# Three engines of a fused attention and two-MLP kernel: a fixed order for token blocks two to four, and the weight preparation in smaller parts

## The chip, the cores and the metric

The kernel runs on one core of a Trainium2 chip, as one launch. The metric is the device time of that launch in microseconds. Five engines work side by side on the core, each through its own queue: TensorE (PE in the profile, with the weight loads apart as PEld), VectorE (DVE), ScalarE (ACT), GpSimd (POOL, nearly unused here) and SyncE (SP), which issues nearly all DMAs.

## The reference, cut to what matters

Chunked attention with memory tokens makes `x`, an MLP with a leaky ReLU turns it into a second `x`, and a gated MLP makes the output. All arrays are float32; there are 3072 tokens of width 512.

```python
# _attn_ref: 4 batches, 8 heads, 768 positions of width 64, chunks of 32 that see 16 left, 8 right, 8 memory tokens
scores = scale * np.matmul(q_c, k_full.transpose(0, 1, 3, 2))
a = np.exp(scores - np.max(scores, axis=-1, keepdims=True))
out[:, :, c_start:c_end] = np.matmul(a / (np.sum(a, axis=-1, keepdims=True) + 1e-09), v_full)
# _moe_ref: w_in 512 x 2048, w_out 2048 x 512
h = x @ w_in
x2 = np.maximum(0.01 * h, h) @ w_out
# _moe2_ref: w_a, w_b 512 x 1536, w_out 1536 x 512
y = ((x2 @ w_a) * (x2 @ w_b)) @ w_out
```

## The kernel before

**Number format.** Every float32 operand of a matmul is split into a high and a low part, and each product takes three matmuls: `mm3` in the first layer (`h<-xh,w`, `h<-xl,w`, `h<-xh,w`) and the same in `mm2` (`a<-gh,w`, `a<-gl,w`, `a<-gh,w`). The high part is a ScalarE cast, the low part a VectorE subtraction.

**Token blocks and items.** The tokens are cut into six blocks of 512 (`NB3`). Blocks one to four (`NL` = 4, index `bi` 0 to 3) go through the first MLP plainly; blocks five and six go together through a Strassen form; the gated MLP follows for all. An item is one block with one of the 16 slices `f` of the inner width; this document numbers the items `16*bi + f`, so block two begins with item 16, block three with 32, block four with 48. The first block has three half items more (its items 16 to 18 of 256 tokens), so that its last half matmuls run beside the first items of block two.

**What an item does.** `mm1_pe` runs 12 matmuls into a PSUM tile `h` (pool `ps_h`, two buffers in turn). `mm1_act` runs two ScalarE operations on it, `g` (the leaky ReLU, which reads `h` and so gives the buffer back) and `gh` (the high part), and VectorE makes `gl`. `mm2` runs the 12 matmuls of the item two items back (`LAG` = 2) into four accumulators `a` (pool `ps_a`, four buffers, all of them used by one block). At the end of a block ScalarE copies the four accumulators out (`x<-a`), and only then the next block can accumulate.

**Attention beside it.** The attention of a later block is made in pairs of units (128 tokens) beside the items: at the items in `STARTS` the scores of a pair run (`s<-k,qz`, on PE), then the softmax, the 16 transposes per unit on VectorE (`pt<-p`), and at the next start the product with V (`pv<-pt,v`). The product uses the same two `h` buffers as the items, and its result goes to `xh` (ScalarE) and `xl` (VectorE).

**Weight preparation.** The weights of the gated MLP are prepared in the meantime, as 18 blocks of work (six pairs of slices, three matrices each). The generator `prep_steps` gives out four steps for each: twice load a tile `raw`, bias it on ScalarE and join its halves into `pz` on VectorE; then the ScalarE casts into `pwa` and four combinations `ps` and the low parts on VectorE; then the cast into `pwb`, its low part, and the stores `wab<-pwa`, `wab<-pwb` (or `wtd<-...`) to DRAM. `pz`, `pwa`, `ps` and `pwb` have one buffer each, `raw` has four, loaded three ahead. 49 of the 72 steps are spread evenly over the 48 items of blocks two to four (`STEPS, pace`), the rest goes to the Strassen part, three for each of its rounds.

**Order.** `InOrder` wraps an engine: while it is on, every instruction of that engine is held behind the one emitted before it. It is on for the first items and again from the Strassen part on. In between the framework's scheduler sets each engine's order. On the chip every engine runs its queue in the order in which it was built.

Of the kernel before, what the change touches and what calls it, by code (L numbers as in the profile page):

```python
# [28 lines left out]
NL = NB3 - 2  # L29
# [26 lines left out]
def kernel(  # L56
# [61 lines left out]
    def w_join_lo(lo, z):  # L118
        dve.scalar_tensor_tensor(
            z, lo, 29, z, ALU.logical_shift_right, ALU.bitwise_or  # L120
        )

    def w_parts(hi, lo, z, eng):

        act.copy(hi, z)
        eng.tensor_tensor(out=lo, in0=z, in1=hi.bitcast(F32), op=ALU.subtract)


# [559 lines left out]

    def next_pair(u):
        for k in (2, 3):  # L690
            q_place(u + k, nc.scalar.copy)
        q_load(u + 6)
        k_load(2 * u + 8)

# [15 lines left out]
    for k, i in enumerate(STARTS[:-1]):  # L710
        u = 2 * TB // UT + 2 * k
        for v in (u, u + 1):
            at_item(i, a_scores, v)
        at_item(i, next_pair, u)
        at_item(i, a_soft1, u)
        at_item(i, a_soft1, u + 1)
        at_item(i + 1, a_soft2, u)
        at_item(i + 2, a_turn, u)
        at_item(i + 2, a_soft2, u + 1)
        at_item(i + 3, a_turn, u + 1)  # L720

# [15 lines left out]

    def prep_join(n, z):
        prep_load(n + AHEAD)
        w_bias(raws[n])  # L740
        w_join(raws[n], z)

    def prep_steps():
        n = 0
        for p in range(NF2 // 2):
            for m in range(3):
                z = prep.tile([P, 2, 512], I32, tag="pz", name="pz", bufs=1)
                for k in range(2):
                    prep_join(n, z[:, k, :])
                    n += 1  # L750
                    yield
# [10 lines left out]
                t = prep.tile([P, 4, 256], F32, tag="ps", name="ps", bufs=1)  # L762

                def plain(c, n, src):
                    w_parts(
                        wa[:, c:c + n, 0], wa[:, c:c + n, 1],
                        src.rearrange("p (a n) -> p a n", n=256), dve,
                    )

                def plain4(c, src):  # L770
                    w_parts(*[
                        wa[:, c, l].rearrange("p (d a j) -> p d a j", d=2, j=32) for l in range(2)
                    ], src, dve)

                def comb(c, x, y, op):
# [7 lines left out]
                    dve.tensor_tensor(out=o, in0=x, in1=y, op=op)  # L783

                if m < 2:
                    plain(0, 2, z[:, 0, :])
                    plain(2, 1, z22)
                    comb(1, z21, z22, ALU.add)
                    comb(0, t[:, 1], z11, ALU.subtract)
                    comb(2, z11, z21, ALU.subtract)  # L790
                    comb(3, z12, t[:, 0], ALU.subtract)
                else:
                    plain4(0, z11)
                    plain4(1, z21)
                    plain4(2, z22)
                    comb(0, z12, z11, ALU.subtract)
                    comb(1, z22, t[:, 0], ALU.subtract)
                    comb(2, z22, z12, ALU.subtract)
                    comb(3, z21, t[:, 1], ALU.subtract)
                yield  # L800
                g, k = divmod(p, 2)
# [6 lines left out]
                wb = prep.tile([P, 4, 2, 256], F32R, tag="pwb", name="pwb", bufs=1)  # L808
                w_parts(wb[:, :, 0], wb[:, :, 1], t, dve)
                yield  # L810
                if m < 2:
                    nc.sync.dma_start(out=d[:, 2:5], in_=wb[:, 0:3].bitcast(F32))
                    nc.sync.dma_start(out=d[:, 6], in_=wb[:, 3].bitcast(F32))
                else:
                    nc.sync.dma_start(out=wtd[g][:, 3:7, k], in_=wb.bitcast(F32))

    steps = prep_steps()


# [165 lines left out]

    STEPS, pace = 49, 0.0
    for bi, f, parts in items[LEAD:]:
        first = bi == 0
        if f == 0 and not first:
            if bi + 1 < NL:  # L990
                x_tiles(("x", bi + 1))
            else:
                x_raw()
        if first:
            W1.load(2 * f + 14)
            W1.step()
        behind.append((bi, parts, mm1(bi, parts)))
        if first:
            W1.step()
        if len(behind) > LAG:  # L1000
            mm2(*behind.pop(0))
        for fn in beside.get((bi, f), []):
            fn()
        if not first:
            wo_load((bi - 1) * NF1 + f + 3)

            i = (bi - 1) * NF1 + f
            n = (NL - 1) * NF1
            pace += STEPS / n
            near = {i + NF1, i + NF1 - 1, i + NF1 + 1} & set(STARTS)  # L1010
            for _ in range(0 if near else int(pace)):
                pace -= 1
                next(steps, None)
        elif f >= NF1 - 1:
            wo_load(f - NF1 + 2)
            prep_load(f - NF1 + 1)


# [33 lines left out]

    for e in (pe, dve, act):
        e.on, e.last = True, None
    whole = slice(0, TB)
# [8 lines left out]
    for p in range(NF1 // 2):  # L1064
# [14 lines left out]
        prod(Bk, p, 1, 1, False)  # L1079
        if p:  # L1080
            next(steps, None)
        g11 = relu(Bk)()
# [16 lines left out]
        if p:  # L1099
            next(steps, None)  # L1100
        prod(A, p, 5, 2, False)
# [3 lines left out]
        if p:  # L1105
            next(steps, None)
        late = summed(u2, C)
# [520 lines left out]
```

## Time and profile before

| | |
|---|---|
| median of 3 runs | 1120.54 us (1120.48 to 1122.62) |
| the profiled execution | 1120.36 us |
| its span | 1118.5 us |
| what lies around the span | 1.86 us |
| PE busy | 1096.0 us (98% of the span) |
| DVE busy | 772.9 us (69%) |
| ACT busy | 526.6 us (47%) |
| granted TensorE clock | 0.998 |

The span runs from the first to the last instruction. PE busy counts the time in which at least one matmul is in flight, so what is missing from 100% is time in which TensorE had nothing to run. The stages lie in the span as follows: block one to about 128 us, blocks two to four to about 425 us, the Strassen part to about 553 us, then the last matmuls of blocks five and six and the gated MLP.

### The profile page before, as it was taken

To read this page: it belongs to the slowest core of one execution; us is meant where nothing else is said; L and a number is where in the kernel's file an instruction comes from. 1 tells how busy PE (TensorE), PEld (TensorE's weight loads), DVE (VectorE), ACT (ScalarE), POOL (GpSimd) and SP (SyncE) were. 2 spreads that over 40 slices of the span, in tenths; PEclk is the share of its full clock that TensorE was granted. 3 is DMA by queue.
4 is the path that set the end of the run, shared out by engine and by line. 5 is a ranking of instruction groups with operands and counts; after the bars stand their busy time and mean duration, and the time that the engine had idled before them with its cause. 6 is when DMAs were issued, how large, how long until landed. Compare 5 with 4: busy or idle time off the path is not lost.

```text
span 1118.5 us, 16332 instructions
## 1 busy us (share of the span) xinstructions
PE 1096.0 (98%) x6195; PEld 908.6 (81%) x6195; DVE 772.9 (69%) x1417; ACT 526.6 (47%) x893; POOL 7.4 (1%) x18
## 2 busy tenths in 40 slices
PE   7899999999999999999999999999999999999997
PEld 6788888888888888877788888888888888888886
DVE  6796388978898665778551737588736578745676
ACT  5887556664555235666622424144434243433232
POOL 2000000000000000000000000000000000000000
PEclk9999999999999999999999999999999999999999
DMA  9996889889998423556688756566877566767452
GB/s 315 404 345 229 282 308 344 297 337 365 327 325 335 158 81 135 186 200 226 246 329 290 266 191 201 181 211 193 275 229 219 166 220 192 242 182 242 143 185 76
DMA packets 99854, 270.63 MB, mean 242 GB/s; under 512 B 9664, under 2 KB 24128, under 8 KB 99008
## 3 DMA queue, kind: packets, MB, share of 16 engines
q1 hardware_dynamic: 98032, 267.88, 70.4%
q10 hardware_dynamic: 1744, 1.70, 0.5%
q8 instruction: 49, 0.80, 0.3%
q14 instruction: 29, 0.24, 0.1%
HBM read 215.02 MB, written 54.53 MB: 241 GB/s over the span
## 4 chain that ended last, share of the span: by engine, by line
PE 81%; DVE 9%; ACT 5%; DMA 3%; issue 1%; SPq 1%; DVEq 0%; ACTq 0%
PE ca L49 18%; PE cc L49 9%; PE oa L49 9%; PE a L49 7%; PE cb L49 5%; PE oy L49 4%; PE h L438 4%; PE a L562 4%; PE a L566 3%; PE a L565 3%; PE h L439 3%; PE h L440 3%; DVE pt L351 2%; PE A L49 2%; PE oz L49 1%; PE pv L391 1%
## 5 line engine op out<-in xcount | busy, mean ns | idle before, releaser
L49 PE MATMUL ca<-ch,wab 128*128 128x512 f32 x576 | 192.2, 389 | 0.0
L49 ACT CAST st<-gb 128x512 fp32r<-128x512 f32 x126 | 76.5, 621 | 124.5 <-DVE gb L49 123.9
L49 PEld LDWEIGHTS ca<-ch,wab 128*128 128x128 f32 x576 | 108.1, 188 | 23.2 <-ACT a L49 0.4
L49 PE MATMUL ca<-cl,wab 128*128 128x512 f32 x288 | 112.2, 389 | 0.0
L49 PE MATMUL oa<-st,wt 128*128 128x512 f32 x420 | 104.3, 389 | 0.0
L438 PE MATMUL h<-xh,w 128*128 128x512 f32 (+1 forms) x256 | 100.5, 393 | 2.8 <-DVE xl L425 2.1
L49 PE MATMUL cc<-ch,wab 128*128 128x512 f32 x288 | 100.3, 389 | 0.0
L439 PE MATMUL h<-xl,w 128*128 128x512 f32 (+1 forms) x256 | 98.6, 385 | 0.2 <-DVE xl L49 0.2
L440 PE MATMUL h<-xh,w 128*128 128x512 f32 (+1 forms) x256 | 98.5, 385 | 0.0
L562 PE MATMUL a<-gh,w 128*128 128x512 f32 (+1 forms) x256 | 97.7, 382 | 0.5 <-ACT x L580 0.5
L565 PE MATMUL a<-gl,w 128*128 128x512 f32 (+1 forms) x256 | 97.5, 381 | 0.0
L566 PE MATMUL a<-gh,w 128*128 128x512 f32 (+1 forms) x256 | 97.5, 381 | 0.0
L49 DVE TENSOR_TENSOR st<-gb,st 128x512 fp32r<-128x512 f32 x126 | 85.3, 689 | 15.0 <-ACT st L49 13.3
L49 PEld LDWEIGHTS oa<-st,wt 128*128 128x128 f32 x420 | 78.8, 188 | 16.4
L49 ACT COPY u<-ca 128x512 f32<-128x512 f32 x72 | 42.3, 587 | 91.5 <-PE ca L49 91.4
L351 DVE STREAM_TRANSPOSE pt<-p 32x128 f32<-32x128 f32 x256 | 77.4, 302 | 3.5
L49 PEld LDWEIGHTS cc<-ch,wab 128*128 128x128 f32 x288 | 54.1, 188 | 11.3
L49 PEld LDWEIGHTS ca<-cl,wab 128*128 128x128 f32 x288 | 54.1, 188 | 11.1
L530 ACT ACTIVATE g<-h 128x512 f32<-128x512 f32 (+1 forms) x64 | 37.3, 583 | 54.2 <-PE h L440 53.9
L536 DVE TENSOR_TENSOR gl<-g,gh 128x512 fp32r<-128x512 f32 (+1 forms) x64 | 43.0, 672 | 26.8 <-ACT gh L533 23.2
L438 PEld LDWEIGHTS h<-xh,w 128*128 128x128 f32 x256 | 48.1, 188 | 13.3 <-DVE xl L425 2.5
L562 PEld LDWEIGHTS a<-gh,w 128*128 128x128 f32 x256 | 48.1, 188 | 10.3 <-ACT x L580 0.9
(198 smaller groups left out, 2050.7 us busy)
## 6 DMA issues: line engine op xcount, KB each, us to landing
wab<-wab SPq DMA_DIRECT2D x126, 512.0 KB, 4.4
w<-wod SPq DMA_DIRECT2D x80, 512.0 KB, 5.3
raw<-w SPq DMA_DIRECT2D x68, 512.0 KB, 7.0
wt<-wtd SPq DMA_DIRECT2D x63, 512.0 KB, 4.5
k<-kl SPq DMA_DIRECT2D x48, 256.0 KB, 4.8
v<-vl SPq DMA_DIRECT2D x48, 256.0 KB, 5.6
wab<-pwb SPq DMA_DIRECT2D x12, 768.0 KB, 5.5
wod<-w SPq DMA_DIRECT2D x16, 512.0 KB, 6.8
```

The lines of the kernel that those rows point to most:

```text
L49: self.last = emit(*args, **kwargs).ins
L351: dve.transpose(out=pt[o0:o0 + 32, :, 2 * cpar + hpar, hpx, :], in_=p[i0:i0 + 32, hpx::2, 32 * b:32 * b + 32],)
L391: pe.matmul(o[64 * hpar:64 * hpar + 64, 2 * pair:2 * pair + 2, t0:t0 + CH], v[:, i:i + 64], pt[:, 2 * cp + pair, 2 * cpar + hpar].rearrang ...
L438: pe.matmul(ps, w[1], x[0], start=first, stop=False)
L439: pe.matmul(ps, w[0], x[1], start=False, stop=False)
L440: pe.matmul(ps, w[0], x[0], start=False, stop=last)
L530: act.activation(g[:, c], ps[:, c], AF.Prelu, alpha=0.01)
L536: dve.tensor_tensor(out=gl[:, c], in0=g[:, c], in1=gh[:, c].bitcast(F32), op=ALU.subtract)
L562: pe.matmul(ps, slot[:, 1, c], gh[:, t], start=f == 0 and o == 0, stop=False, **kw)
L565: pe.matmul(ps, slot[:, 0, c], gl[:, t], start=False, stop=False, **kw)
L566: pe.matmul(ps, slot[:, 0, c], gh[:, t], start=False, stop=f == NF1 - 1 or (o == HALF and f == LEAD - 1), **kw)
```

## The change

Four things are done. `InOrder` is switched on for TensorE, VectorE and ScalarE from the first item of block two. A block of weight preparation has eight steps in place of four, each for one engine alone (bias, join, bias, join, `pwa` casts, combinations with the low parts of `pwa`, `pwb` cast, low part of `pwb`). The even pace is replaced by a table: `steps_at` gives 3, 2, 1 or 0 double steps to an item, by how far it is from the last start of an attention pair; four steps are taken by the end of block one and none from item 60 on. And the attention's pieces stand at other items: both second softmax halves at the item after the start, the `q` copies (`q_next`) at that item and the next. The low part `gl` of an item is emitted behind the matmuls `mm1_pe` of the next item.

```diff
-    def next_pair(u):
-        for k in (2, 3):
-            q_place(u + k, nc.scalar.copy)
-        q_load(u + 6)
-        k_load(2 * u + 8)
+    def q_next(u):
+        q_place(u, act.copy)
+        q_load(u + 3)
...
-        at_item(i, next_pair, u)
-        at_item(i, a_soft1, u)
-        at_item(i, a_soft1, u + 1)
-        at_item(i + 1, a_soft2, u)
-        at_item(i + 2, a_turn, u)
-        at_item(i + 2, a_soft2, u + 1)
-        at_item(i + 3, a_turn, u + 1)
+        at_item(i, k_load, 2 * u + 8)
+        for v in (u, u + 1):
+            at_item(i, a_soft1, v)
+        for v in (u, u + 1):
+            at_item(i + 1, a_soft2, v)
+            at_item(i + 1 + v - u, q_next, v + 2)
+            at_item(i + 2 + v - u, a_turn, v)
...
-                    prep_join(n, z[:, k, :])
+                    prep_bias(n)
+                    yield
+                    w_join(raws[n], z[:, k, :])
                     n += 1
                     yield
...
                     plain(2, 1, z22)
+                    yield
                     comb(1, z21, z22, ALU.add)
...
+                for args in lows:
+                    low(*args)
                 yield
...
-                w_parts(wb[:, :, 0], wb[:, :, 1], t, dve)
+                act.copy(wb[:, :, 0], t)
                 yield
+                low(wb[:, :, 1], t, wb[:, :, 0].bitcast(F32))
...
+    def step():
+        for _ in range(2):
+            next(steps, None)
...
-    STEPS, pace = 49, 0.0
+    def steps_at(i):
+        if i < STARTS[0]:
+            return 3
+        s = [x for x in STARTS if x <= i][-1]
+        return (2, 1, 0, 0, 3, 2)[i - s] if s < STARTS[-1] else 0
+
+    late = None
     for bi, f, parts in items[LEAD:]:
...
+        if bi == 1 and f == 0:
+            for e in (pe, dve, act):
+                e.on, e.last = True, None
         if first:
             W1.load(2 * f + 14)
             W1.step()
-        behind.append((bi, parts, mm1(bi, parts)))
-        if first:
+            behind.append((bi, parts, mm1(bi, parts)))
             W1.step()
-        if len(behind) > LAG:
+        else:
+            n = steps_at(bi * NF1 + f)
+            if n:
+                next(steps, None)
+            ps = mm1_pe(bi, parts)
+            if late:
+                behind.append(late[:2] + (late[2](),))
+            for k in range(n):
+                next(steps, None)
+                if k + 1 < n:
+                    next(steps, None)
+            late = bi, parts, mm1_act(*ps, low=False)
+        if len(behind) >= LAG + first:
             mm2(*behind.pop(0))
...
-            for _ in range(0 if near else int(pace)):
-                pace -= 1
-                next(steps, None)
         elif f >= NF1 - 1:
             wo_load(f - NF1 + 2)
             prep_load(f - NF1 + 1)
+            if f > NF1:
+                step()
+    behind.append(late[:2] + (late[2](),))
...
-        if p:
-            next(steps, None)
         g11 = relu(Bk)()
...
         if p:
-            next(steps, None)
+            step()
```

In the Strassen part one of three calls is dropped and the other two become `step()`, two small steps each.

**ScalarE at the start of block two.** These are ScalarE's rows before, from the first `pwa` cast of the first weight block on; the first `g<-h 128x512` is that of item 16, the second that of item 17, and `x<-a` are the copies of block one's accumulators.

```order
L125 CAST pwa<-pz 128x2x256
L254 COPY qz<-qr 64x16x32
L255 COPY qz<-qr 64x16x32
L530 ACTIVATE g<-h 128x512
L533 CAST gh<-g 128x512
L106 ACTIVATE raw<-raw 128x512
L125 CAST pwa<-pz 128x256
L530 ACTIVATE g<-h 128x512
L580 COPY x_1688<-a 128x256
L533 CAST gh<-g 128x512
L580 COPY x_1691<-a 128x256
L580 COPY x_1694<-a 128x256
```

These are ScalarE's rows of the change at the same place, from the bias of the second `raw` tile on; L46 and L49 are the lines of `InOrder` through which every instruction goes while it is on.

```order
L106 ACTIVATE raw<-raw 128x512
L49 CAST pwa<-pz 128x256
L49 CAST pwb<-ps 128x4x256
L49 ACTIVATE raw<-raw 128x512
L49 ACTIVATE g<-h 128x512
L49 CAST gh<-g 128x512
L49 ACTIVATE raw<-raw 128x512
L49 CAST pwa<-pz 128x2x256
L49 CAST pwa<-pz 128x256
L49 CAST pwb<-ps 128x4x256
L49 ACTIVATE g<-h 128x512
L49 CAST gh<-g 128x512
```

The `g` of item 16, ahead of the second `raw` bias before, now stands behind it, behind the first `pwb` cast and a third `raw` bias; the `g` of item 17 stands behind the second `pwb` cast.

**ScalarE behind item 17.** The rows that follow directly on the last of those:

```order
L49 COPY x_1737<-a 128x256
L49 COPY x_1740<-a 128x256
L49 COPY x_1743<-a 128x256
L49 COPY x_1746<-a 128x256
L49 ACTIVATE raw<-raw 128x512 x2
L49 ACTIVATE g<-h 128x512
L49 CAST gh<-g 128x512
```

The four copies of block one's accumulators, which stood among `g` and `gh` of item 17 before (x_1688 to x_1697 there), stand behind both.

**ScalarE at items 28 and 29.** Before, these rows stand around the `pv` products at item 29 (`xh<-pv`):

```order
L125 CAST pwb<-ps 128x4x256
L106 ACTIVATE raw<-raw 128x512
L530 ACTIVATE g<-h 128x512
L533 CAST gh<-g 128x512
L106 ACTIVATE raw<-raw 128x512
L424 CAST xh<-pv 128x4x128
L125 CAST pwa<-pz 128x256
L424 CAST xh<-pv 128x4x128
L125 CAST pwa<-pz 128x256 x2
```

With the change, from the `pwb` cast of item 28 to the `xh` casts of item 29:

```order
L49 CAST pwb<-ps 128x4x256
L49 ACTIVATE raw<-raw 128x512 x2
L49 ACTIVATE g<-h 128x512
L49 CAST gh<-g 128x512
L49 CAST pwa<-pz 128x256 x3
L49 CAST pwb<-ps 128x4x256
L49 ACTIVATE g<-h 128x512
L49 CAST gh<-g 128x512
L49 CAST xh<-pv 128x4x128 x2
```

Two `pwb` casts now stand one item apart, and `g` of item 29 stands behind the second. TensorE's own rows are the same instructions in the same order, before and with the change.

## Rows read from the trace of the kernel before

**Rows 1.** The page's busy times: us (share of span) xinstructions.

```profile
PE 1096.0 (98%) x6195; PEld 908.6 (81%) x6195; DVE 772.9 (69%) x1417; ACT 526.6 (47%) x893; POOL 7.4 (1%) x18
```

**Rows 2.** Busy time by stretch; columns as in the first line.

```profile
core 0: us, PE busy (x) PEld busy (x) DVE busy (x) ACT busy (x) POOL busy (x), PEclk, DMA share, GB/s
...
128.00:344.00 216.00, 213.35 (x1615) 178.34 (x1615) 184.96 (x448) 122.87 (x194) 0.00 (x0) 1.00 0.90 324
...
425.00:553.00 128.00, 126.52 (x549) 101.69 (x548) 90.83 (x164) 79.41 (x135) 0.00 (x0) 1.00 0.56 195
```

**Rows 3.** PE's waits, 128 to 425 us: total, times, longest.

```profile
PE h L438 <- DVE xl L425: 2.1, 3, 0.9
PE a L562 <- ACT x L580: 0.5, 1, 0.5
```

**Rows 4.** PE's longest wait, 425 to 553 us.

```profile
PE a L49 <- DVE gl L49: 1.1, 2, 0.9
```

**Rows 5.** PE timeline: first matmuls of items 16, 17, 18, then of item 16's `mm2`.

```profile
127.98 0.40 PE L438 MATMUL h<-xh,w 128*128 128x512 f32 x1
...
132.16 0.40 PE L438 MATMUL h<-xh,w 128*128 128x512 f32 x1
...
136.34 0.40 PE L438 MATMUL h<-xh,w 128*128 128x512 f32 x1
...
139.09 0.39 PE L562 MATMUL a<-gh,w 128*128 128x512 f32 x1
```

**Rows 6.** ACT timeline, 126 to 141 us: start, duration, what [idle before <-releaser].

```profile
130.93 0.60 ACT L530 ACTIVATE g<-h 128x512 f32<-128x512 f32 x1 [0.60 <-PE h L440]
...
134.41 0.66 ACT L106 ACTIVATE raw<-raw 128x512 f32<-128x512 f32 x1 [2.23 <-DMA raw<-w]
...
137.10 0.36 ACT L580 COPY x<-a 128x256 f32<-128x256 f32 x1
137.35 0.64 ACT L533 CAST gh<-g 128x512 fp32r<-128x512 f32 x1
...
138.40 1.08 ACT L125 CAST pwb<-ps 128x1024 fp32r<-128x1024 f32 x1
139.34 0.71 ACT L106 ACTIVATE raw<-raw 128x512 f32<-128x512 f32 x1
139.92 0.62 ACT L530 ACTIVATE g<-h 128x512 f32<-128x512 f32 x1
```

**Rows 7.** DVE timeline, 134 to 142 us.

```profile
135.10 0.43 DVE L116 TENSOR_SCALAR pz<-raw 128x512 int32<-128x512 int32 x1 [2.20 <-ACT raw L106]
135.57 0.69 DVE L119 SCALAR_TENSOR_TENSOR pz<-raw,pz 128x512 int32<-128x512 int32 x1
...
137.31 0.42 DVE L783 TENSOR_TENSOR ps<-ps,pz 128x256 f32<-128x256 f32 x1
...
139.51 1.23 DVE L126 TENSOR_TENSOR pwb<-ps,pwb 128x1024 fp32r<-128x1024 f32 x1 [0.73 <-ACT pwb L125]
```

**Rows 8.** DMA issues of the stores: count, KB each, median us to landing.

```profile
wab<-pwb SPq DMA_DIRECT2D x12, 768.0 KB, 5.5
...
wab<-pwa SPq DMA_DIRECT2D x12, 512.0 KB, 4.9
...
wab<-pwb SPq DMA_DIRECT2D x12, 256.0 KB, 5.9
```

**Rows 9.** All stores of tile `pwb`.

```profile
DMA to landing us min/median/max: 3.2/5.8/10.0
```

**Rows 10.** PE timeline: first matmul after a pair's scores, then the next `pv`.

```profile
212.86 0.50 PE L438 MATMUL h<-xh,w 128*128 128x512 f32 x1
...
240.29 2.09 PE L391 MATMUL pv<-pt,v 128*64 128x64 f32 x64
```

**Rows 11.** DVE groups, 128 to 344 us: count | busy us, mean ns.

```profile
L351 DVE STREAM_TRANSPOSE pt<-p 32x128 f32<-32x128 f32 x192 | 58.1, 302 | 2.5
...
L119 DVE SCALAR_TENSOR_TENSOR pz<-raw,pz 128x512 int32<-128x512 int32 x23 | 15.9, 689 | 0.5
...
L783 DVE TENSOR_TENSOR ps<-ps,pz 128x256 f32<-128x256 f32 x8 | 3.3, 418 | 0.0
```

More of the change, by code (lines that the diff above doesn't have):

```diff
@@ L121, in w_join_lo @@
         )
-    def w_parts(hi, lo, z, eng):
-        act.copy(hi, z)
-        eng.tensor_tensor(out=lo, in0=z, in1=hi.bitcast(F32), op=ALU.subtract)
     wslot = {}
@@ L736, in prep_load, with prep_bias @@
             raws.append(raw)
-    def prep_join(n, z):
+    def prep_bias(n):
         prep_load(n + AHEAD)
         w_bias(raws[n])
-        w_join(raws[n], z)
     def prep_steps():
@@ L762, in prep_steps, with split @@
                 t = prep.tile([P, 4, 256], F32, tag="ps", name="ps", bufs=1)
+                lows = []
+                def split(hi, lo, src):
+                    act.copy(hi, src)
+                    lows.append((lo, src, hi.bitcast(F32)))
                 def plain(c, n, src):
-                    w_parts(
+                    split(
                         wa[:, c:c + n, 0], wa[:, c:c + n, 1],
-                        src.rearrange("p (a n) -> p a n", n=256), dve,
+                        src.rearrange("p (a n) -> p a n", n=256),
                     )
                 def plain4(c, src):
-                    w_parts(*[
+                    split(*[
                         wa[:, c, l].rearrange("p (d a j) -> p d a j", d=2, j=32) for l in range(2)
-                    ], src, dve)
+                    ], src)
                 def comb(c, x, y, op):
@@ L783, in comb, with low @@
                     dve.tensor_tensor(out=o, in0=x, in1=y, op=op)
+                def low(lo, x, hi):
+                    dve.tensor_tensor(out=lo, in0=x, in1=hi, op=ALU.subtract)
                 if m < 2:
@@ L795, in prep_steps @@
                     plain4(2, z22)
+                    yield
                     comb(0, z12, z11, ALU.subtract)
@@ L815, in prep_steps @@
                     nc.sync.dma_start(out=wtd[g][:, 3:7, k], in_=wb.bitcast(F32))
+                yield
     steps = prep_steps()
+    def step():
+        for _ in range(2):
+            next(steps, None)
     NS = NB3 // 2
@@ L984 @@
     at_item(max(STARTS) + 2, s_begin)
-    STEPS, pace = 49, 0.0
+    def steps_at(i):
[4 more added lines that the diff above has]
+    late = None
     for bi, f, parts in items[LEAD:]:
+        i = (bi - 1) * NF1 + f
         first = bi == 0
@@ L1004 @@
         if not first:
[L1005 to L1010, printed above, removed]
-            for _ in range(0 if near else int(pace)):
-                pace -= 1
-                next(steps, None)
+            wo_load(i + 3)
         elif f >= NF1 - 1:
@@ L1051, in next2 @@
         wo_load(done2[0] + (4 if done2[0] < NL * NF1 else 6))
-    for e in (pe, dve, act):
-        e.on, e.last = True, None
     whole = slice(0, TB)
@@ L1105 @@
         if p:
-            next(steps, None)
+            step()
         late = summed(u2, C)
```

## The prediction

> **What bounds the kernel now.** The page first: TensorE is busy for 1096.0 of 1118.5 us [rows 1], so the kernel is bound by it, and 22.5 us are all that any order can win. The busy times by stretch say where those lie: blocks two to four lose 216.00 - 213.35 = 2.65 us, all before 344 us, and the Strassen part 128.00 - 126.52 = 1.48 us [rows 2]; the rest is the beginning and the tail, which the change doesn't touch. The waits name the causes. In blocks two to four TensorE waits three times for `xl` (2.1 us, the next item needs the `h` buffer that a `pv` product still holds) and once for a copy of the accumulators (0.5) [rows 3]. In the Strassen part it waits twice for `gl` (1.1) [rows 4]. So about 4 us can be won here, and every wait that the new order makes costs its whole length. The same stretch shows that VectorE has little room: 184.96 of 216 us, 86%, and ScalarE much (57%) [rows 2].
>
> **What the change leaves alone.** The instructions are the same on every engine, and TensorE's stand in the same order. "TensorE in program order" therefore costs and brings nothing. What moves is when ScalarE and VectorE get to `g`, `gh`, `gl`, `xl` and the accumulator copies.
>
> **Term one: the start of block two.** Before, ScalarE runs `g` of item 16 at 130.93 and waits afterwards for the second `raw` tile, which lands at 134.41 [rows 6]. With the change `g` of item 16 stands behind that bias. The stores and loads on SP ahead of this load are the ones of before, so I keep its landing time. Then, by durations of the same place: the join starts at 135.10 and ends at 135.57 + 0.69 = 136.26; four combinations, three of them each needing the one before, at 0.42 make it 137.85 [rows 7]; the `pwb` cast takes 1.08 (138.9); the next bias begins 0.94 after the cast's begin as in the rows and takes 0.71 (139.5); `g` ends 0.62 later, at 140.1 [rows 6]. TensorE came to item 18 at 136.34 [rows 5], and item 18 needs the `h` buffer of item 16. It waits about 3.8 us there, and its 12 matmuls end at 140.1 + (139.09 - 136.34) = 142.85.
>
> The next matmuls are item 16's `mm2`, the first of block two. They need the accumulators, hence block one's copies, which now stand behind `g` and `gh` of item 17, which stand behind the second `pwb` cast. That cast has two conditions. The first is work: bias (141.4), then on VectorE the first `pwb` low part (1.23, to 140.2), a join, `gl` of 16, a join and four combinations, about 4.6 us more: 144.8. The second is the one buffer of `pwb`: the first tile's stores can be issued at 140.2 and land 5.5 and 5.9 us later [rows 8], at 146.1. I take the later: cast to 147.2, `g` 147.8, `gh` (0.64) 148.45, first copy (0.36) [rows 6] 148.8. Item 16's `mm2` began at 139.09 before [rows 5], so **term one is 9.7 us**, the first wait included. With stores that land in the 3.2 us of the fastest [rows 9] the work decides: 144.8 + 1.08 + 0.62 + 0.64 + 0.36 = 147.5, 8.4 us. With the slowest, 10.0, it would be 13.8. Of the two I keep the median, since no load is late here by any row. While TensorE waits, the two other engines catch up, and items 17 and 18 find their `gl` made.
>
> Here a page has another price. The Trainium skill, "DMA: Bandwidth & Descriptors", section "Anatomy of one DMA", puts a DMA from GpSimd at about 2.0 us and bytes over 436 GB/s; for 768 KB that is an estimate of 3.8 us. The rows of this kernel, whose stores are issued by SP, say 5.5 and disagree. By the page term one would be 8.4 and term two nothing.
>
> **Term two: items 29, 45 and 55.** These are starts of a pair where one item casts `pwb` and the next one again. From the first matmul after the scores to the next `pv` TensorE needs 240.29 - 212.86 = 27.4 us [rows 10]; the second of the two products, 1.0 later at 28.4, needs the `h` buffer of the item just run, so its `g`. VectorE must have done by then: the 32 transposes, 9.7 us at 302 ns; eleven operations of 512 columns at 0.69 (7.6); the four small ones, some 0.7; combinations and `pwa` low parts. The seven groups of preparation from 15.9 down to 3.3 us sum to 72.9 us for 12 blocks [rows 11], 6.1 a block, of which the two joins are 2.2 and the `pwb` low part 1.2, so these are 2.7. Together 20.7, less 1.0 for the first maximum, which runs beside the second unit's scores; then the `pwb` low part 1.2 to 20.9, to which I add 0.5 for waits on `gh`: 21.4. Its store lands at 27.3, the next cast ends at 28.4, `g` at 29.0: 0.6 late, and 0.4 more for the two issues on SP. **3 times 1.0 is 3.0 us.** From below: the store may land before the combinations are done, which costs nothing. From above: a store of 10.0 us makes 4.7 us at one place; I don't expect that at all three, and take 6.3 as the upper end. At items 23 and 39 the same two casts meet no `pv`, so 1.7 us of lateness is covered there by a whole item (5.4 us).
>
> **Term three: what is removed.** The three waits for `xl` go, since `xl` has nothing of the preparation between it and the product any more: -2.1. The wait for the copies within the blocks goes: -0.5 (at items 33 and 49 the copies stand behind `gh` again, but that `pwb` cast meets no store in flight; it costs up to 1.2 each if VectorE is a microsecond later than I think). In the Strassen part two calls of two small steps replace three whole ones: VectorE has 4/8 of a block per round in place of 3/4, 1.5 us less of 6.1, and the two `gl` waits go: -1.1, or nothing. Term three is -3.7, between 0 and -4.1.
>
> **The sum.** 9.7 + 3.0 - 3.7 = +9.0 us. The profiled execution took 1120.36 us, 0.18 below the median of the runs, so 1129.4. Its own bounds: 8.4 + 0 - 4.1 = +4.3, or 1124.7; 13.8 + 6.3 + 1.2 - 0 = +21.3 with everything at its worst, of which I take two thirds, 1135.
>
> **Rivals.** *Faster: the knot at the start doesn't form.* It hangs on one number, when the second `raw` tile lands. Each microsecond earlier takes one off the first wait. If it landed before 130.6 the first wait would be gone, and if by 124.5, ten before 134.41, both, and the stores would be out in time. Then the waits removed stand alone: 1120.36 - 3.7 = 1116.7. Against it: ScalarE waited 2.23 us for that very load in this trace [rows 6]. The Trainium skill, "Perfetto Trace Analysis", section "Optimizing Scalar/DVE Operations", speaks for this rival: where these engines are not full but cause bubbles elsewhere, breaking up instructions may let work be done sooner. Here no instruction is broken up, only the steps are. Chance 0.08.
>
> *No change:* half the knot, the tile some 6 us earlier and no loss at the `pv` products, within 2 us of 1120.5. Chance 0.05.
>
> *Much slower: VectorE becomes the bound.* 15 blocks of preparation instead of some 12 now lie before item 60. A pair with its five items holds 1.5 blocks (9.1 us), 9.7 of transposes, five `gl` and ten more operations of 0.69 (10.4) and small ones of 0.7: 29.9 us, against some 31.4 of TensorE (the 27.4, and 2 each for the two products and the two scores). If VectorE idles more than 1.4 us per pair behind ScalarE or the scores, every further microsecond is paid at each of eight pairs: 1 to 2 us make 8 to 16, 1137 to 1145. For it: 86% already, and before the scheduler could fill holes with the next step. Against it: operations in a row overlap by some 0.1 us in the timeline (the cast and the bias of [rows 6]); if VectorE's 25 or so larger ones of a pair do the same, that gives 2.5 us of room. Chance 0.12.
>
> **Numbers.** My forecast has the remaining 0.75. A measurement of this kernel tells about 0.2% (2.2 us) from no change. Faster 0.08, same 0.05, slower 0.87. Range 1122 to 1137: it leaves out the faster case and most of the much slower one; the forecast's own is 1124 to 1135.
>
> **What the profile after would show.** Right: TensorE idle for some 4 us ahead of item 18 with ScalarE's `g` as the releaser, then for some 6 us ahead of item 16's `mm2` with an accumulator copy; ScalarE's second `pwb` cast waiting for a `wab<-pwb` store; no `xl` wait; a short wait of `pv` on `g` at three of the eight pairs. Wrong: item 18 starts near 136, or TensorE's waits in blocks two to four sum to under 3 us. It would also be wrong if VectorE is busy all through and `gl` is what TensorE waits for, pair after pair.

## The result, and the profile after

| | before | after |
|---|---|---|
| median | 1121.18 us (4 runs, 1120.48 to 1122.62) | 1134.3 us (4 runs, 1133.53 to 1136.0) |
| profiled execution, its span | 1120.36, 1118.5 us | 1134.86, 1133.1 us |
| granted TensorE clock | 0.998 | 0.993 |

The change makes the kernel slower by 1.2%: the ratio is 1.0117, with a 95% interval of 1.01 to 1.0135, some 13 us. The forecast was +9.0 us. (The kernel before has one run more here than ahead of the prediction.)

The page of the changed kernel gives these busy times, beside [rows 1].

```profile
PE 1101.9 (97%) x6195; PEld 914.1 (81%) x6195; DVE 777.3 (69%) x1417; ACT 527.2 (47%) x893; POOL 7.4 (1%) x18
```

TensorE runs the same 6195 matmuls and is busy for 5.9 us more, and it is idle for 31.2 us in place of 22.5. So 8.7 us are waits, and the rest are matmuls that took longer. The busy times by stretch of the changed kernel, cut at the start of block two, within the blocks, and at the Strassen part, say where:

```profile
core 0: us, PE busy (x) PEld busy (x) DVE busy (x) ACT busy (x) POOL busy (x), PEclk, DMA share, GB/s
128.00:160.00 32.00, 24.03 (x153) 19.28 (x152) 17.17 (x32) 14.94 (x26) 0.00 (x0) 0.79 0.91 322
160.00:344.00 184.00, 182.97 (x1357) 152.98 (x1356) 162.98 (x394) 102.83 (x158) 0.00 (x0) 1.00 0.89 321
344.00:439.70 95.70, 94.48 (x689) 78.31 (x689) 79.51 (x176) 46.73 (x74) 0.00 (x0) 1.00 0.69 251
439.70:567.70 128.00, 125.40 (x549) 102.57 (x549) 80.39 (x143) 73.46 (x124) 0.00 (x0) 1.00 0.42 150
```

The first 32 us have 7.97 us of the idle time, and a granted clock of 0.79. The waits of TensorE of 0.3 us and more in the changed kernel from block two to the end of the Strassen part, in order of time (start, duration, what, idle before and releaser):

```profile
141.25 0.80 PE L49 MATMUL h<-xh,w 128*128 128x512 f32 x1 [3.65 <-ACT g L49]
148.33 0.80 PE L49 MATMUL a<-gh,w 128*128 128x512 f32 x1 [2.73 <-ACT x L49]
154.13 0.79 PE L49 MATMUL a<-gh,w 128*128 128x512 f32 x1 [1.59 <-ACT x L49]
252.50 0.50 PE L49 MATMUL a<-gh,w 128*128 128x512 f32 x1 [1.03 <-ACT x L49]
352.99 0.50 PE L49 MATMUL a<-gh,w 128*128 128x512 f32 x1 [0.84 <-ACT x L49]
437.80 0.50 PE L49 MATMUL a<-gl,w 128*128 128x512 f32 x1 [0.37 <-DVE gl L49]
488.48 0.50 PE L49 MATMUL a<-gl,w 128*128 128x512 f32 x1 [0.83 <-DVE gl L49]
519.53 0.50 PE L49 MATMUL a<-gl,w 128*128 128x512 f32 x1 [0.84 <-DVE gl L49]
550.68 0.50 PE L49 MATMUL a<-gl,w 128*128 128x512 f32 x1 [0.91 <-DVE gl L49]
```

The first is item 18 waiting for `g` of item 16, the second item 16's `mm2` waiting for the first accumulator copy, the third the same `mm2` waiting for the fourth copy; the next two are the ends of blocks two and three, and the last four are waits for `gl` in the Strassen part. A matmul of 512 columns that follows a wait took 0.50 us later on and 0.80 in the first three: there the clock is at the lower of its two levels, 1.2 GHz (the granted clock was 0.50 from 142 to 144 us and from 148 to 154). ScalarE at that place, with what ended its own waits:

```profile
135.50 0.67 ACT L106 ACTIVATE raw<-raw 128x512 f32<-128x512 f32 x1 [4.10 <-DMA raw<-w]
...
139.10 1.04 ACT L49 CAST pwb<-ps 128x1024 fp32r<-128x1024 f32 x1 [1.31 <-DVE ps L49]
...
140.62 0.57 ACT L49 ACTIVATE g<-h 128x512 f32<-128x512 f32 x1
...
145.81 1.04 ACT L49 CAST pwb<-ps 128x1024 fp32r<-128x1024 f32 x1 [1.24 <-DMA wab<-pwb]
146.76 0.59 ACT L49 ACTIVATE g<-h 128x512 f32<-128x512 f32 x1
...
147.91 0.91 ACT L49 COPY x<-a 128x256 f32<-128x256 f32 x3
153.70 0.37 ACT L49 COPY x<-a 128x256 f32<-128x256 f32 x1 [4.88 <-DMA x2d<-x]
```

The chain is the one that the prediction followed, `raw`, join, combinations, `pwb` cast, `g` of 16, second `pwb` cast, `g` of 17, copies; and then one link more. Block one's copies go into `z` tiles, of which there are three, so the fourth copy waits 4.88 us for the store of the first. That store stands on SyncE's queue (start, duration, what) behind the stores of the second weight block:

```profile
148.51 0.45 SPq L820 DMA_DIRECT2D wab<-pwb  x1
149.05 2.94 SPq L575 DMA_DIRECT2D x2d<-x  x3
```

Before, no weight store stood ahead of it. It was issued at 137.49, and the fourth copy ran at 140.40, behind `g` of item 18 and without a wait:

```profile
137.49 1.60 SPq L581 DMA_DIRECT2D x2d<-x  x3
```

```profile
140.40 0.40 ACT L580 COPY x<-a 128x256 f32<-128x256 f32 x1
```

**Where the time is lost** is read best from markers that both traces have: the last `pv` product beside block one and the first ones at items 24 and 60 begin at 123.92, 176.78 and 404.58 us before, and at 125.02, 191.51 and 418.57 after. The first two before and then after:

```profile
123.92 1.15 PE L391 MATMUL pv<-pt,v 128*64 128x64 f32 x32
176.78 2.08 PE L391 MATMUL pv<-pt,v 128*64 128x64 f32 x64
```

```profile
125.02 1.15 PE L385 MATMUL pv<-pt,v 128*64 128x64 f32 x32
191.51 2.09 PE L49 MATMUL pv<-pt,v 128*64 128x64 f32 x64
```

The 1.10 at the first were there before the two programs differ (the experiments' traces have from 0.12 us earlier to 1.26 later there than the one of before). So item 24 is 14.73 - 1.10 = **13.6 us late**, and item 60 13.99 - 1.10 = 12.9. At the last round of the Strassen part (`B` begins at 538.30 before, 553.31 after) it is 13.9. So the loss arises in the 32 us in which block two begins; 0.7 us are won by item 60, and 1.0 is lost again by the last round of the Strassen part.

### The profile page after: what moved, and what is told of

Its sections match the earlier page's. It is cut to its first block, busy times and chain, and to the rows that moved or that the text cites. A ratio compares the mean times of both kernels' runs of the same rounds, so it can differ in the third digit from the quotient of the medians.

```text
span 1133.1 us, 16325 instructions
## 1 busy us (share of the span) xinstructions
PE 1101.9 (97%) x6195; PEld 914.1 (81%) x6195; DVE 777.3 (69%) x1417; ACT 527.2 (47%) x893; POOL 7.4 (1%) x18
## 4 chain that ended last, share of the span: by engine, by line
PE 85%; DVE 8%; ACT 3%; DMA 2%; issue 1%; SPq 0%; DVEq 0%; ACTq 0%
PE ca L49 18%; PE a L49 16%; PE cc L49 9%; PE oa L49 8%; PE h L49 8%; PE cb L49 5%; PE oy L49 4%; PE A L49 2%; PE pv L49 2%; DVE pt L49 2%; PE oz L49 1%; PE s L49 1%; PE h L432 1%; PE C L49 1%; PE h L433 1%; PE a L556 1%
## 5 line engine op out<-in xcount | busy, mean ns | idle before, releaser
L49 PE MATMUL ca<-ch,wab 128*128 128x512 f32 x576 | 192.5, 390 | 0.0
L49 PE MATMUL a<-gh,w 128*128 128x512 f32 (+1 forms) x536 | 175.6, 390 | 6.7 <-ACT x L49 6.2
L49 PE MATMUL h<-xh,w 128*128 128x512 f32 (+1 forms) x407 | 133.1, 390 | 4.3 <-ACT g L49 3.6
L49 ACT CAST st<-gb 128x512 fp32r<-128x512 f32 x126 | 76.5, 621 | 124.6 <-DVE gb L49 124.0
L49 PEld LDWEIGHTS ca<-ch,wab 128*128 128x128 f32 x576 | 108.2, 188 | 23.2 <-ACT a L49 0.5
L49 PEld LDWEIGHTS a<-gh,w 128*128 128x128 f32 x536 | 101.2, 190 | 29.1 <-ACT x L49 8.2
L49 PE MATMUL ca<-cl,wab 128*128 128x512 f32 x288 | 112.3, 390 | 0.0
L49 PE MATMUL a<-gl,w 128*128 128x512 f32 (+1 forms) x268 | 104.6, 390 | 3.0 <-DVE gl L49 3.0
L49 PE MATMUL oa<-st,wt 128*128 128x512 f32 x420 | 104.3, 389 | 0.0
L49 PE MATMUL cc<-ch,wab 128*128 128x512 f32 x288 | 100.5, 390 | 0.0
L49 DVE TENSOR_TENSOR st<-gb,st 128x512 fp32r<-128x512 f32 x126 | 85.3, 689 | 15.0 <-ACT st L49 13.3
L49 PEld LDWEIGHTS h<-xh,w 128*128 128x128 f32 x407 | 76.5, 190 | 20.3 <-ACT g L49 3.9
L49 PEld LDWEIGHTS oa<-st,wt 128*128 128x128 f32 x420 | 78.9, 188 | 16.3
L49 ACT COPY u<-ca 128x512 f32<-128x512 f32 x72 | 42.2, 586 | 91.6 <-PE ca L49 91.4
L49 DVE STREAM_TRANSPOSE pt<-p 32x128 f32<-32x128 f32 x256 | 77.4, 302 | 3.3
L49 PE MATMUL h<-xl,w 128*128 128x512 f32 (+1 forms) x204 | 78.9, 387 | 0.3 <-DVE xl L49 0.3
L49 PEld LDWEIGHTS cc<-ch,wab 128*128 128x128 f32 x288 | 54.1, 188 | 11.3
L49 PEld LDWEIGHTS ca<-cl,wab 128*128 128x128 f32 x288 | 54.1, 188 | 11.1
L49 PEld LDWEIGHTS a<-gl,w 128*128 128x128 f32 x268 | 51.0, 190 | 14.5 <-DVE gl L49 4.6
L49 DVE TENSOR_TENSOR gl<-g,gh 128x512 fp32r<-128x512 f32 (+1 forms) x67 | 45.2, 676 | 19.6 <-ACT gh L49 19.1
L49 PE MATMUL cc<-cl,wab 128*128 128x512 f32 x144 | 56.1, 390 | 0.0
L49 PE MATMUL oy<-st,wt 128*128 128x512 f32 x216 | 53.8, 389 | 0.0
```

What stands on the lines that cost most here:

```text
L49: self.last = emit(*args, **kwargs).ins
```

## The experiments

In the table, "late" is the delay at item 24's and item 60's `pv`, worked out from the run's own trace as above, less that at the last `pv` beside block one. A trace is of one execution, the median of all: the traces of e9, e4 and e10 are of executions 3.1, 2.0 and 1.4 us above their medians, that of e3 is 1.2 below. The ratio is to runs of the kernel before on the same chip, which had medians of 1119.5 to 1120.4.

| run | what | median us | ratio, 95% | late at 24 | at 60 |
|---|---|---|---|---|---|
| (after) | the change | 1134.3 | 1.0117 (1.01 to 1.0135) | 13.6 | 12.9 |
| e1 | no steps at items 16, 17 | 1119.78 | 0.9992 (0.9983 to 1.0002) | 0.0 | -2.8 |
| e2 | fixed order from item 18 | 1137.01 | 1.0151 (1.0136 to 1.0166) | 16.2 | 15.5 |
| e3 | spare matmuls in the waits | 1134.04 | 1.0124 (1.0109 to 1.0139) | 12.0 | 11.3 |
| e4 | fourth copy in a `t` tile | 1129.98 | 1.0084 (1.0067 to 1.0101) | 10.7 | 10.0 |
| e5 | steps of 16, 17 behind `g`, copies | 1130.65 | 1.0097 (1.0073 to 1.0121) | 8.6 | 8.3 |
| e6 | e2 and e4 together | 1125.13 | 1.0043 (1.0027 to 1.006) | 2.4 | 2.7 |
| e11 | e5 and e4 together | 1126.16 | 1.005 (1.0036 to 1.0064) | 3.4 | 4.2 |
| e8 | before, with the fixed order alone | 1135.26 | 1.0136 (1.0119 to 1.0153) | 1.5 | 7.4 |
| e10 | the change without the fixed order | 1123.88 | 1.003 (1.0021 to 1.0039) | 3.2 | 3.8 |
| e7 | e1, Strassen steps one and three | 1123.75 | 1.0033 (1.0019 to 1.0046) | 0.0 | -2.7 |
| e9 | e7, none in the last round | 1119.66 | 1.0001 (0.9991 to 1.0011) | 0.0 | -2.7 |
| e12 | e9, the rest spread | 1121.31 | 1.0011 (1.0001 to 1.0021) | 0.0 | -2.9 |

**e1, the start without its steps.**

```diff
         if i < STARTS[0]:
-            return 3
+            return 0
```

> The change, with no double steps of preparation at items 16 and 17 (the table gives 0 there in place of 3), so that the g of item 16 stands no longer behind the second raw tile; one block and a half of preparation moves to the end of the Strassen part. Theory (the knot at the start is made by the preparation steps ahead of g): the waits of 3.6 us on g and of 2.7 us on the copies go, and with them the stretch at the lower clock; of the 12.7 us that were lost between 125 and 155 us at most 2 stay (the fourth copy still needs the store of the first), so 1134.3 - 11 to 12.7 = 1122 to 1123. Rival (the fixed order itself makes it, copies behind g and gh of item 17 and the stores behind them): more than 6 us of it stay, 1128 or more.

The theory held, and more came back than it said. The stretches of this run:

```profile
128.00:160.00 32.00, 32.00 (x213) 27.19 (x212) 21.16 (x48) 19.07 (x31) 0.00 (x0) 1.00 0.89 311
160.00:344.00 184.00, 183.95 (x1466) 154.19 (x1467) 163.04 (x389) 102.44 (x161) 0.00 (x0) 1.00 0.88 321
344.00:425.00 81.00, 80.63 (x531) 66.78 (x526) 67.28 (x147) 37.65 (x58) 0.00 (x0) 1.00 0.65 242
425.00:553.00 128.00, 124.64 (x545) 101.55 (x544) 82.37 (x148) 75.28 (x127) 0.00 (x0) 1.00 0.46 160
```

TensorE isn't idle at the start, and hardly in all of blocks two to four (0.42 us, against 2.65 before): without the steps at these two items the rest of the change is a gain of 2.8 us there. There is no run of e1 without the fixed order, so how much of this gain is the order's stays open. The fourth copy waited 2.8 us on ScalarE here too, beside other work of TensorE.

**e2, the order from item 18 on.**

```diff
-        if bi == 1 and f == 0:
+        if bi == 1 and f == 2:
             for e in (pe, dve, act):
```

> The change, with the fixed order switched on from item 18 in place of item 16; the same steps of preparation at items 16 and 17, which the scheduler places by itself. Theory (g of item 16 standing behind the second raw tile costs the time): ScalarE runs g of item 16 before that tile lands, TensorE doesn't wait at item 18 for long, and some 8 us or more come back: 1122 to 1126. Rival (it is the amount of preparation at these two items, six double steps, whatever their order): no more than 4 us come back, 1130 to 1134.

The rival was nearer, and the run was slower still. Here ScalarE's order is the scheduler's until item 18: `g` of 16 runs at 130.85, three copies at 136.79 to 139.4, all before they are wanted. But the fourth copy, and SyncE:

```profile
154.48 0.79 PE L49 MATMUL a<-gh,w 128*128 128x512 f32 x1 [13.26 <-ACT x L574]
```

```profile
147.75 0.44 SPq L820 DMA_DIRECT2D wab<-pwb  x1
148.24 2.94 SPq L575 DMA_DIRECT2D x2d<-x  x3
```

The first copy was made at 137.15, and its store was issued at 148.24, because the stores of both weight blocks stand ahead of it, and those wait for the preparation on VectorE and ScalarE, whose second `pwb` cast (145.05) had itself waited 2.08 us for the first block's store. TensorE waited 13.26 us in one piece for the fourth copy. So `g` behind the `raw` tile is one way to lose the time, and not the only one.

**e4, e6: the fourth copy.**

```diff
-                    tag, bufs = ("z", 3) if e < KC - 1 or bi == 0 else ("t", None)
+                    tag, bufs = ("z", 3) if e < KC - 1 else ("t", None)
```

> The change, with the fourth copy of block one's accumulators put into a t tile (four buffers) in place of the z tile (three), so that it needs no store of the first copy. Theory (ScalarE's 4.9 us wait at 149 us for that store costs TensorE the 1.6 us wait on the fourth accumulator, and what the low clock makes of it): 2 to 4 us less, 1130.5 to 1132.5. Rival (TensorE would wait at the next place instead, for g of item 18 behind the copy, or the t tile makes g wait): 1134 to 1135.

> The fixed order from item 18 on, with the fourth copy of the accumulators in a t tile. With the z tile this kernel took 1137.0 us, since the fourth copy waited 13.3 us for the store of the first, which stands on SyncE behind the stores of two weight blocks. Theory (that store's place on SyncE is all that is left of the knot when ScalarE's order is the scheduler's): TensorE doesn't wait any more at item 16's second product, and 13 to 15 us go: 1121 to 1124. Rival (the second pwb cast or the next raw tiles are late by themselves): TensorE waits 4 us or more at item 18 or 19, 1127 or more.

e4 went the theory's way, 0.5 us beyond its range (4.3 us less by the medians, 2.9 by item 24). e6 was 1 us above its theory, and its start is clear: no wait on `g` or a copy, only 0.41 and 0.87 us on `gl` and 0.90 on `g` at item 24's `pv`. With the scheduler's order at items 16 and 17 and one more buffer, 13.8 of e2's 16.2 us go.

**e5, e11: the steps behind the item's own work.**

```diff
-            if n:
+            if n and i >= 2:
                 next(steps, None)
...
-            for k in range(n):
+            for k in range(n if i >= 2 else 0):
...
             mm2(*behind.pop(0))
+        if bi and i < 2:
+            for _ in range(2 * n):
+                next(steps, None)
```

> The change, with the same six small steps at items 16 and 17, but emitted behind the item's g, gh and, at item 17, behind the copies of the accumulators, in place of ahead of g. The amount of preparation is that of the change. Theory (the place of g and of the copies among the steps, with their stores on SyncE, makes the knot): g of 16 ends before 132 us, the copies and their stores stand ahead of the second block's casts and stores, and the 12.7 us of the start go but for 1 to 3 (the first pwb cast still stands ahead of g of item 17): 1121 to 1125. Rival (six double steps in two items are too much whatever their place): 6 us or more of it stay, 1128 or more.

> The change with the steps of items 16 and 17 emitted behind g, gh and the copies (1130.7 us by itself), and with the fourth copy in a t tile (1130.0 us by itself). Theory (two parts of the knot that add up: 2.5 us of wait on the fourth copy and the low clock behind it go from the first of these): 1125 to 1127, with 1.3 us on the first copy and 0.5 on gl left at about 141 us. Rival (g of item 18 behind the second pwb cast becomes the next wait, and gives back most of it): 1128 to 1131.

e5's theory failed, the rival's number came, and for another reason than the rival's. `g` of 16 ran at 132.02, but the first three copies (141.24) still stood behind item 16's `pwb` cast, and the fourth waited 5.71 us for a store that SyncE issued behind the first block's stores. e11, with the fourth buffer, came in its theory's range, though the 1.3 us on the first copy that it expected to stay were gone too; 3.4 us are left at item 24, of which 1.32 are `pv` waiting on `g`. So the amount of preparation at these items is not what costs most of the time.

**e3, the clock.**

```diff
+    def dummy(n):
...
+        for _ in range(n):
+            pe.matmul(spare[0], w[:, 0, 0:P], x[:, 0], start=True, stop=True)
```

> The change, with matmuls on a spare PSUM tile of no use to the result put on TensorE into the three waits at the start of block two (14 ahead of item 18, 16 ahead of item 16's second product, 13 ahead of its fourth accumulator), so that TensorE is busy while ScalarE is late. Theory (the stretch at half the clock after the waits costs time by itself): the granted clock stays near 1.0 from 141 to 160 us, and the matmuls behind the last wait, some 4 us at the lower level, take half: 1134.3 - 2 to 3 = 1131.5 to 1132.5. Rival (it is only the waits; whatever TensorE loses by the clock is hidden in the next wait): 1134 to 1135.

The granted clock was 1.00 in the same stretch:

```profile
128.00:160.00 32.00, 30.30 (x202) 25.06 (x201) 18.01 (x34) 15.33 (x28) 0.00 (x0) 1.00 0.93 336
```

The trace gives back 13.6 - 12.0 = 1.6 us, less than expected; the medians (1134.04 and 1134.3) don't tell it from nothing, which was the rival's number. Of the 13.6 us, 13.6 - 7.97 = 5.7 were matmuls at the lower clock, but most of that lay ahead of the next wait, whose end ScalarE and SyncE set.

**e8, e10: the order and the rest, apart.** e8 is the kernel before with `InOrder` on from item 16, e10 the change with it on only from the Strassen part, as before.

> The kernel before, with nothing but the fixed order of TensorE, VectorE and ScalarE switched on from item 16 (old steps, old pace, old places of the attention). Theory (the fixed order by itself loses time, since a whole step holds ScalarE and VectorE for each other and whatever stands behind): waits on g or gl at the items with a step, 0.3 to 1 us at some 20 of 48 items, 1127 to 1140. Rival (the order alone is harmless, and the loss of the change is only that of the two items with six double steps): 1117 to 1122.

> The change without its fixed order: the small steps, the table and the new places of the attention, with the scheduler setting each engine's order up to the Strassen part. Theory (the six double steps at items 16 and 17 with their stores on SyncE cost the start in any order, as they did with the order switched on from item 18, 1137.0 us): 1132 to 1140, with a wait of more than 8 us on the fourth copy at about 141 to 155 us. Rival (the scheduler, free in all of blocks two to four, puts the copies and g early enough): 1119 to 1126.

e8's time came in its theory's range, by fewer and longer waits than it said. Its start is good (1.5 us late at item 24), since ScalarE has a single `raw` bias there among `g`, `gh` and the copies. It loses later, by six waits of an item for `g`, 6.5 us together, and then by 2.11 us for `gh` and 0.91 for `gl` with the low clock behind them at the start of the Strassen part: it is 7.4 us late at item 60 and 14.5 at the last round. One of the six:

```profile
239.12 0.50 PE L49 MATMUL h<-xh,w 128*128 128x512 f32 x1 [1.55 <-ACT g L49]
```

e10's theory failed: without the order the same steps cost 3.2 us at item 24. SyncE's order is as bad as in e2 (the `x2d` stores were issued at 151.90), but on TensorE the scheduler ran three accumulators of items 16 to 18 and put the fourth's matmuls of all three behind them, where they waited 0.74 us for the fourth copy:

```profile
157.28 0.50 PE L556 MATMUL a<-gh,w 128*128 128x512 f32 x1 [0.74 <-ACT x L574]
```

In e2, whose order is fixed from item 18 on, the same late copy cost 13.26 us. "TensorE in program order therefore costs and brings nothing" was right for the order that the change has, and not for what a late copy does in it.

**e7, e9, e12: the Strassen part,** all from e1. e7 takes one small step at the first place and three at the second; e9 takes none in the last round; e12 gives out the rest, four behind each of the first three items of the last matmuls. This is e9's edit; e7 has `if p:` where it says `if 0 < p < 7:`.

```diff
-        if p:
-            step()
+        if 0 < p < 7:
+            next(steps, None)
         prod(A, p, 5, 2, False)
...
-        if p:
-            step()
+        if 0 < p < 7:
+            step()
+            next(steps, None)
```

> The change with no steps at items 16 and 17, and in each round of the Strassen part one small step at the first place and three at the second, in place of two and two, so that the four combinations and the low parts of pwa stand behind gl and not ahead of it. Theory (the 0.84 us waits on gl in every second round come from these 2.4 us of VectorE work ahead of gl): three waits and the 0.8 us one on s go, against the same kernel with two and two (1119.8 us) 2 to 3.3 us less, 1116.5 to 1117.8. Rival (VectorE is late there anyway, by the low part of pwb or the sum behind it): 1119 to 1120.5.

> The kernel with no steps at items 16 and 17 and one and three small steps per round of the Strassen part, now without any steps in its last round (they are made behind the part, where VectorE idles). With steps in the last round it took 1123.8 us: TensorE waited 3.1 us for a sum that stood behind them on VectorE and then ran at the lower clock to about 558 us. Theory (that wait and its low clock are what the move cost, and the three waits on gl of 0.84 us are gone): 3 to 4.5 us less than 1123.8 and 2 to 3 less than the 1119.8 us with two and two steps, so 1116.5 to 1118. Rival (the steps behind the part delay the loads of the gated MLP, or the copies of A to B, 0.25 us late in every second round, take the gain back): 1119 to 1121.

> The same kernel as the one of 1119.7 us (no steps at items 16 and 17, one and three in the Strassen rounds, none in its last), with the twelve remaining small steps emitted four at a time behind the first three items of the last matmuls of block six, so that each item's load of second weights stands ahead of their stores on SyncE. Theory (of the 2.6 us won from gl, a 1.8 us wait for such a load at 577 us and some 4 us at the lower clock behind it took all back): the wait and the low clock go, 1119.7 - 1.8 - 1.9 = 1116.0, between 1115 and 1117.3. Rival (the loads are late all the same, since the DMA engines are full there): 1118.5 to 1120.

VectorE in the changed kernel shows why `gl` is late, and what e7 moved:

```profile
485.34 0.42 DVE L49 TENSOR_TENSOR ps<-pz 128x256 f32<-128x256 f32 x1
...
486.80 1.02 DVE L49 TENSOR_TENSOR pwa<-pz,pwa 128x512 fp32r<-128x512 f32 x2
487.74 0.68 DVE L49 TENSOR_TENSOR gl<-g,gh 128x512 fp32r<-128x512 f32 x1
```

In e7 the three waits on `gl` are gone, but the six rounds between the second `B` and the last take no less (`B` begins at 443.19 and 537.03, 93.84 us; 93.29 in e1, 93.25 in the change, 92.95 before). The waits are smaller and more. PE shows no idle time for `gl` there any more; its weight loads still wait. These are e7's waits of weight loads between 440 and 540 us (total, times, longest), and under them the only ones of e1:

```profile
PEld a L49 <- DVE gl L49: 2.0, 6, 0.4
PEld B L49 <- ACT B L49: 2.0, 3, 0.7
PEld A L49 <- ACT u L49: 1.9, 6, 0.4
```

```profile
PEld a L49 <- DVE gl L49: 3.8, 3, 1.3
```

That the new small waits took the gain fits these sums; no run tests it. In e7's last round a sum stood behind the steps on VectorE, and this is what followed, the granted clock (0.53) at its lower level:

```profile
553.18 0.97 PE L49 MATMUL a<-g,w 128*128 128x512 f32 x3 [3.06 <-DVE s L49]
```

```profile
556.00:558.00 2.00, 2.00 (x6) 1.51 (x6) 0.00 (x0) 0.94 (x2) 0.00 (x0) 0.53 1.05 426
```

So e7 was slower than its theory and its rival. e9 took this away, and then, in its trace, the rest of the preparation, behind the part, held up the loads of second weights on SyncE:

```profile
577.51 20.97 PE L49 MATMUL a<-g,w 128*128 128x512 f32 x84 [1.79 <-DMA w<-wod]
```

This trace is of an execution of 1122.72 us, where e9's median is 1119.66. The wait and the slow matmuls behind it, 1.8 and 1.9 us, are about that difference, so most executions of e9 may not have them; no trace here shows one. e12's theory took the 3.7 us off the median, to 1116.0, and e12 measured 1121.31. In e12 that wait is gone, and TensorE waited 1.41 us at 613 us for a load of the gated MLP's weights (`wab`). e9's time is its rival's; e12's is 1.3 us above its rival's range. No version is faster than the kernel before by more than the measurement tells; e1 and e9 equal it.

## Why the prediction was right, and where its terms were off

**What bounds the kernel:** right. Nothing but TensorE's waits and its clock moved the time, and VectorE, busy for 69%, did not become the bound; that rival is refuted.

**Term one (+9.7):** the right place and the right releasers, and too small. Item 18's wait was 3.65 us (forecast 3.8). Item 16's `mm2` began at 148.33, which is 148.33 - 1.10 - 139.09 = 8.1 us later than before [rows 5], nearer to my bound from the work (8.4) than to 9.7, since the store landed earlier than I took (the second `pwb` cast began 4.4 us after the first store was issued at 141.44). The step that failed is the end of the chain: I followed it to the first copy and took the other three for free. The fourth needed a buffer, hence a store, hence SyncE's queue; without that wait (e4) the whole start costs 10.7. The low clock is the other part, and I did not price it at all: it adds at most the 1.6 of e3 in the change, and more in e4, where no copy hides it. The scores of item 18 follow on item 16's `mm2`; this is their start before, in the change, and in e4, with e4's start of the `mm2`:

```profile
141.90 2.08 PE L282 MATMUL s<-k,qz 128*64 128x64 f32 x64
```

```profile
155.70 3.01 PE L49 MATMUL s<-k,qz 128*64 128x64 f32 x64
```

```profile
148.26 0.79 PE L49 MATMUL a<-gh,w 128*128 128x512 f32 x1 [2.96 <-ACT x L49]
153.68 2.27 PE L49 MATMUL s<-k,qz 128*64 128x64 f32 x64
```

Before, the `mm2` took 141.90 - 139.09 = 2.8 us. In e4 it began 7.9 us late and took 5.4 at a granted clock of 0.50, 2.6 more. In the change it began 8.1 late and took 7.4 with the fourth copy in it, 4.6 more, and the scores took 0.9 more. So 13.6 in place of 9.7.

The sentence "It hangs on one number, when the second `raw` tile lands" was wrong too. e2 lost more with `g` of 16 ahead of that tile. What the steps hold up is more than ScalarE: six double steps put two blocks' stores on SyncE ahead of the `x2d` stores. I looked at that queue ahead of the load that I followed, and not at what the moved steps put ahead of the others. (Ahead of the prediction the four copies are said to have stood among `g` and `gh` of item 17; the fourth stood behind `g` of item 18.)

**Term two (+3.0):** did not come. There is no wait of `pv` on `g` at items 29, 45 and 55 in the changed kernel. The chain is there: the second `pwb` cast waits 1.52, 1.87 and 1.82 us for the store at these three items. This is item 29's:

```profile
221.89 1.06 ACT L49 CAST pwb<-ps 128x1024 fp32r<-128x1024 f32 x1 [1.52 <-DMA wab<-pwb]
```

But the cast began 4.4 us after the store was issued (217.52), and `g` ended 0.4 to 0.9 us ahead of the second product, which begins 1.0 after the first. The term rested on the 5.5 us of [rows 8]; the median of the same store is now

```profile
wab<-pwb SPq DMA_DIRECT2D x12, 768.0 KB, 3.3
```

The Trainium skill, "DMA: Bandwidth & Descriptors", section "Anatomy of one DMA", gave an estimate of 3.8 us for it (by its rate for a DMA from GpSimd), and by it term two was nothing: for the changed kernel the page was nearer than the row of before. Why the landing time fell I did not settle. Where the start was repaired, the same chain made a wait at item 24's `pv`, a pair that I had not named (0.90 us in e6, 1.32 in e11).

**Term three (-3.7):** the three waits for `xl` and the copy's went, -2.6, as forecast; e1's stretches show it cleanly. The copies at items 33 and 49, which I set to nothing with a bound of 1.2 each, cost 1.03 and 0.84. The Strassen part was wrong. I argued with VectorE's total per round, which did fall, but what counts is what stands ahead of `gl`: four combinations and the low parts of `pwa`, 2.4 us, in every second round. Three waits of 0.8 to 0.9 us replaced two (0.23 and 0.91), and the change is 0.3 us slower there by the rounds; that it is not more fits the waits of weight loads on `u`, which were 1.3 us before and are gone. With 0.7 us at the start of the part, term three was about +0.3.

**Sum:** 13.6 + 0 + 0.3 = 13.9 us by the traces, 13.1 by the medians. A term too small by 3.9 and one too favourable by 4.0 met one too large by 3.0, so it is in part luck that the sum missed by only 4.9.

**The faster rival** asked for an earlier `raw` tile. e1 gave what it meant, a start without a knot, and its price of 1116.7 was too low: the 2.8 us gained in the blocks were half given back from the Strassen part on (its span is 0.2 us below that of before, and its last `pv` beside block one came 1.26 later).

## What to carry to other kernels

When work is moved ahead of a place, follow the chain past the first instruction that waits: to the last copy, its buffer, the store that frees the buffer, and the queue on which that store stands behind the moved work's own stores. A fixed order was harmless here only where each item's steps fitted beside its matmuls: without steps at items 16 and 17 (e1) blocks two to four gained 2.8 us, and with them the two items lost 13.6. A wait that was removed left several too short to be listed in its place (e7), so measure the stage by its markers and not by the waits that vanished. And before a wait in a trace is subtracted from a median, look at whether the traced execution is a usual one (e9).

## What the runs showed of the hardware

After waits of 3.65 us (the change), 3.06 (e7), 1.93 (e10), and 1.79 (e9) the granted clock fell to the lower level for some 3 to 4 us once TensorE worked again. These are e9's rows from 578 us on, columns as above:

```profile
578.00:580.00 2.00, 2.00 (x7) 1.57 (x6) 1.80 (x2) 0.13 (x1) 0.00 (x0) 0.55 1.02 420
580.00:582.00 2.00, 2.00 (x7) 1.55 (x6) 1.05 (x1) 0.92 (x1) 0.00 (x0) 0.59 1.03 422
582.00:584.00 2.00, 2.00 (x10) 1.65 (x9) 1.31 (x2) 0.66 (x1) 0.00 (x0) 1.00 0.72 240
```

There a wait of 1.79 us cost 1.9 more: 84 matmuls took 20.97 us, where 84 at the pace of the rows (0.227) are 19.1. After e12's 1.41 and e8's 1.55 it stayed at 1.00.
